# Two edits to a hand-ordered attention-and-MLP kernel: later rounding of raw weights at the seam, and later loads for the last projection block

## The chip, the cores and the metric

The kernel runs on one core of a Trainium2 chip. The metric is the device time of one execution in microseconds (us). Engines are named as in the profile: PE (matmul; PEld its weight loads), DVE (vector), ACT (scalar, activation functions), POOL (GpSimd), SP (which here only issues DMAs). Each engine executes its instructions in the order in which the program emitted them, and waits on semaphores for the others.

## The reference

The input is one sequence of 2048 tokens with 576 features, all in 32-bit floats. Output: a gate between full attention (32 heads of 18) and an MLP.

```
g = sigmoid((x * gate_w).sum(-1))
a = softmax(q @ k.T * 18**-0.5) @ v   per head, then @ wo
b = gelu(layernorm(x) @ w1 + b1) @ w2 + b2      # 576 -> 4608 -> 576
return g * a + (1 - g) * b
```

## The kernel before, in words

Every matrix is used as a rounded high part and the remainder as a low part (the "rounding": an ACT copy to the high part, line 381, then a POOL subtraction for the low part, line 385, booked under the helper's line 176). Products are sums of three matmuls.

**Stages.** Stage A goes over the 4 blocks of 512 input tokens: transposes, q/k projections (groups 0 to 8 of a block, `qk_group`), v projections (groups 9 to 16, `v_group`: even token halves are evicted by ACT, lines 843 and 845, odd ones by DVE, line 847, and stored by SP, line 850), layer-norm outputs y to DRAM. Then comes the main loop: 32 units (16 pairs of heads times 2 halves of the queries) of 16 key chunks each, so 512 steps. A step has score matmuls with exponentials (`s2`, lines 263 and 266), rounds that find row maxima for later units (`s1_round`, lines 223 and 225), and every second step the product with V (`pv`, line 281). Into the gaps between these goes the MLP, a generator whose pieces are pulled one at a time by `fill`; after the MLP the output projection `out_proj` is pulled in the same way. The **seam** is the passage from stage A to the main loop; the **tail** is what follows the last `pv`.

**Slots.** `run_due` counts slots. In stage A it is called by a table: in the last token block once after each of the groups 0 to 8 and twice after each of 9 to 16 (13 slots have passed before that block). In the loop there are 8 slots in two steps, beginning with slot 39. `defer(n, fn)` runs `fn` n slots later. `run_due` also looks through the list `bg` of pieces of background work; one is run when its slot has come and a model of POOL's backlog (sum of modelled operation times minus modelled present) is under its limit: 950 ns for a W1 rounding, 3800 ns for a W2 rounding.

**Raw weights.** In the first token block of the MLP the raw weights are loaded (`load_w1`, line 352, one pair of 128 hidden columns; `load_w2`, line 362, one row chunk), rounded by `split`, used, and stored rounded in DRAM for the other three blocks. One raw buffer R1 serves all W1 pairs, two buffers R2 serve W2 chunks. `LOADED` holds the slot from which a load counts as landed. Only emission order hangs on that slot: the copy itself waits for the transfer, and as ACT runs in order, all that was emitted behind the copy waits too. When a rounding's subtraction is emitted, the load of the next raw piece is deferred by some slots (line 387). The first raw loads are issued within group 2 of the last block; the list is filled at group 9 with W1 0, W2 0 to 3, W1 1 and W1 2. Within group 16 four loads (line 132, `big<-y_scr`) bring the rest of y.

At the seam, PE takes turns between MLP pairs (`h_pair`, matmuls of line 473, two PSUM banks), scores (five banks in rotation) and `pv`. GELU of a pair is a chain of POOL (adds and products), ACT (square, tanh, lines 526 and 524) and POOL steps; its results feed `out_pair` (line 561).

**Tail.** The last unit's `o_store` takes its sums with a copy to DVE's tile `oe`, extracts the denominators (`dn<-oe`, on ACT's queue for the last unit), and 4 slots later `spread` takes the reciprocal (line 305), stores it (line 306) and calls the hook `over`. From then on `ended` is set, outputs leave through ACT's queue, and `load_rest` loads the last rows and denominators of the third and fourth token blocks (lines 1011 and 1016). These two blocks hold the last unit's queries.

`out_proj` works on four blocks of 512 tokens; each has 8 half tiles of 14 matmuls (line 1114, two PSUM banks `ps_w`), evicted by DVE (line 1118) together with gate and MLP result `bt`. Behind each eviction a stage of `normed` for the next block may be emitted, by the table `PLAN`: multiply by the reciprocal denominators (line 1040, DVE), copy (1043, 1046, 1047, ACT), subtract (1050, 1052, DVE). At the start of block b the loads of `bt` for b + 1 are issued, and at the start of block 1 also the attention rows (`load_o(3)`, lines 974 and 977) and denominators (`load_den(3)`, lines 996 and 999) of the fourth block.

Of the kernel before, what the change touches and what calls it, by code (L numbers as in the profile page):

```python
# [23 lines left out]
NB = 4  # L24
# [16 lines left out]
LAND = 8  # L41
# [24 lines left out]
def gated_mix_kernel(ctx: ExitStack, tc: tile.TileContext, x, wqkv, wo, w1, b1, w2, b2, gate_w, out):  # L66
# [68 lines left out]
    slot = [0]  # L135
# [3 lines left out]
    def defer(n, fn):  # L139
        later.append((slot[0] + n, fn))  # L140
# [38 lines left out]
    NU = 2 * NPAIR  # L179
# [108 lines left out]
    def o_store(u, ps):  # L288

        pair, half = unit(u)  # L290
        oe = asm.tile([P, TB], F32, name="oe", bufs=1)
        dn = asm.tile([P, 16], F32, name="dn", bufs=1)
        nc.vector.tensor_copy(oe, ps)
        cols = slice(2 * pair * DH, 2 * (pair + 1) * DH)
        queue = nc.sync if u < NU - 1 else nc.scalar
        queue.dma_start(dn, oe[DH::32, :])
        for h in range(2):
            for qb in range(2):
                c = 32 * (2 * h + qb)
                d = (2 * pair + h) * DH  # L300
                q = half * HALF + qb * TB
                queue.dma_start(ot_scr[0, d:d + DH, q:q + TB], oe[c:c + DH, :])

        def spread():
            nc.vector.reciprocal(dn, dn)
            nc.sync.dma_start(dn_scr[u], dn)
            if u < NU - 1:
                defer(16 if u < NU - 2 else 4, wide)
            else:
                hooks[0]()  # L310

        def wide():
            dst = ot_scr[1, cols, half * HALF:(half + 1) * HALF]
            nc.sync.dma_start(dst.rearrange("(h d) n -> h d n", d=DH), dn_scr[u][:, None, :].to_broadcast([2, DH, HALF]))
            stored.append(u)
        defer(20 if u < NU - 2 else 4, spread)

    rounds = [(u, r) for u in range(NU) for r in range(NR)]
    rounds.reverse()
# [12 lines left out]
    def mlp():  # L332
# [16 lines left out]
        LOADED = {}  # L349
        NQ0 = npair // NB  # L350

        def load_w1(q):

            if (1, q) in LOADED or q >= NQ0:
                return
            LOADED[1, q] = slot[0] + (LAND if looped[0] else LAND - 2)
            fc = chunk(q)[2]
            for h in range(2):
                src = w1[:, (fc + h) * P:(fc + h + 1) * P]
                nc.sync.dma_start(R1[64 * h:64 * h + 64], src.rearrange("(c p) n -> p c n", p=64))  # L360

        def load_w2(c):
            if (2, c) in LOADED or c >= NFC:
                return
            LOADED[2, c] = slot[0] + (LAND if looped[0] else LAND - 2)
            nc.sync.dma_start(R2[c % 2], w2[c * P:(c + 1) * P, :])

        def rounded(dst, src):
# [7 lines left out]
        def split(table, key, pool, shape, raw, src, scr, then):  # L376

            def first():
                LOAD[raw[0]](raw[1])
                t = pool.tile(shape, F32R, name="w" + str(len(shape)))  # L380
                nc.scalar.activation(t[:, 0], src, AF.Copy)  # L381
                bg.insert(0, (any_time, lambda: second(t), queue, 0))

            def second(t):
                pool_op(src.free_size(), nc.gpsimd.tensor_tensor, t[:, 1], src, t[:, 0].bitcast(F32), op=ALU.subtract)
                defer(4 if looped[0] else 26 if raw[0] == 1 else 44, lambda: nc.sync.dma_start(scr, t.bitcast(F32)))
                defer(3 if looped[0] else 2 if raw != (1, 2) else 14, lambda: then(raw[1]))
                table[key] = (t[:, 0], t[:, 1])

            queue = raw[0] ** 2 * SLOT  # L390
            bg.append((lambda: LOADED.get(raw, slot[0] + 1), first, queue, (ROOM if raw[1] > 3 else 0) if raw[0] == 1 else D))
# [552 lines left out]
    def out_proj():  # L944
# [24 lines left out]
        def load_o(b):  # L969

            inflow[0] = slot[0]
            o = x_tile().rearrange("p (c n) -> p c n", c=5)
            cols = slice(b * TB, (b + 1) * TB)
            nc.sync.dma_start(o[:, 0:4, :], ot_scr[0, 0:512, cols].rearrange("(c p) n -> p c n", p=P))
            for h in range(2):
                e = 64 if b < 2 else LAST
                nc.sync.dma_start(o[64 * h:64 * h + e, 4, :], ot_scr[0, 512:512 + e, cols])
            OT[b] = [o]
            done[b] = 0

        def load_den(b):

            while len(stored) < (NU - 2 if b < 2 else NU - 1):
                run_due()
            if b == 0:
                wide = low.bitcast(F32)[:, 0:4, :]
                den = [low.bitcast(F32)[:, c, :] for c in range(5)]
            elif b % 2 == 0:
                wide = KA[0].bitcast(F32).rearrange("p (c n) -> p c n", c=4)
                den = [wide[:, c, :] for c in range(4)] + [QA[2][:, :TB].bitcast(F32)]  # L990
            else:
                tile_ = io.tile([P, 5, TB], F32, name="den", bufs=1)
                wide = tile_[:, 0:4, :]
                den = [tile_[:, c, :] for c in range(5)]
            cols = slice(b * TB, (b + 1) * TB)
            nc.sync.dma_start(wide, ot_scr[1, 0:512, cols].rearrange("(c p) n -> p c n", p=P))
            for h in range(2):
                e = 64 if b < 2 else LAST
                nc.sync.dma_start(den[4][64 * h:64 * h + e], ot_scr[1, 512:512 + e, cols])
            OT[b].append(den)  # L1000
            if ended[0]:
                load_rest(b)
# [3 lines left out]
        def load_rest(b):  # L1006

            o, den = OT[b][:2]
            cols = slice(b * TB, (b + 1) * TB)
            for h in range(2):  # L1010
                nc.sync.dma_start(o[64 * h + LAST:64 * h + 64, 4, :], ot_scr[0, 512 + LAST:576, cols])
            sums = dn_scr[NU - 1][:, (b - 2) * TB:(b - 1) * TB]
            for h in range(2):
                for j in range(2):
                    r = 64 * h + LAST + j * DH
                    nc.sync.dma_start(den[4][r:r + DH], sums[j:j + 1, :].to_broadcast([DH, TB]))
            ready.add(b)

        def load_b(b):
            t0 = len(BT.setdefault(b, []))  # L1020
            bt = io.tile([P, 4 - t0, D], F32, name="bt", bufs=2)
            nc.sync.dma_start(bt, b_scr[b * TB + t0 * P:(b + 1) * TB, :].rearrange("(t p) d -> p t d", p=P))
            BT[b] += [bt[:, t] for t in range(4 - t0)]
# [34 lines left out]
        def over():  # L1058

            ended[0] = True  # L1060
            for b in (2, 3):
                if b in OT and len(OT[b]) > 1:
                    load_rest(b)
        hooks.append(over)
        waiting = []

        def go_on(last):
# [23 lines left out]
        load_b(0)  # L1091
        yield 0
        for b in range(NB):
            if b + 1 < NB:
                load_b(b + 1)
            if b == 1:
                load_o(3)
                load_den(3)
            for t in range(4):
                if b == 0 and t == 1:  # L1100
                    load_o(2)
                    load_den(2)
                tt = 4 * b + t
                tok = slice(t * P, (t + 1) * P)
                res = io.tile([P, D], F32, name="res", bufs=6)
                for n in range(2):
                    cs = slice(n * ND, (n + 1) * ND)
                    ps = psum(ps_w)
                    k = 0
                    for c in range(5):  # L1110
                        while done[b] <= c:
                            run_due()
                        for s_, w_ in ((c, 0), (c, 1), (4 + c, 0)) if c < 4 else ((8, 0), (8, 1)):
                            nc.tensor.matmul(ps[:, :ND], OT[b][2][:, s_, tok], w_part(w_, c)[:, cs], start=(k == 0), stop=(k == 13))  # L1114
                            k += 1
                            if k < 14:
                                yield 122.5
                    nc.vector.scalar_tensor_tensor(res[:, cs], ps[:, :ND], gate[:, tt:tt + 1], BT[b][t][:, cs],
                                                   op0=ALU.mult, op1=ALU.add)
                    if b + 1 < NB:  # L1120
                        waiting.extend((b + 1, stage) for stage in PLAN[b][2 * t + n])
                        go_on(t == 3 and n == 1)
                    yield 122.5
                if ended[0]:
                    nc.scalar.dma_start(out[tt * P:(tt + 1) * P, :], res)
                else:

                    defer(3, lambda res=res, tt=tt: nc.sync.dma_start(out[tt * P:(tt + 1) * P, :], res))
# [100 lines left out]
```

## Time and profile before

| what | us |
|---|---|
| median of 3 runs | 2252.6 (2252.51 to 2253.47) |
| the profiled execution | 2251.12 |
| its span in the profile | 2249.3 |
| granted TensorE clock, mean | 0.997 |
| PE busy | 2223.9 |
| DVE busy | 1648.3 |
| ACT busy | 1425.8 |
| POOL busy | 964.4 |

Rows of a timeline give start, duration, engine, line, operation, output<-inputs, shapes, count of merged instructions, and in brackets the idle time before with what ended it. Rows "A <- B" of the waits give the total, the number and the longest. Rows by stretch give the stretch, then busy time and count of PE, PEld, DVE, ACT and POOL, then the granted TensorE clock, the DMA share and GB/s. DMA rows on SP and ACT's queue show when a transfer was issued, not when it landed.

### The profile page before, as it was taken

The numbers are of one execution on the slowest core, as the hardware profiler recorded it, in microseconds if no ns is written. First come the engines' busy times: TensorE is split into PE (matmuls) and PEld (weight loads), VectorE is DVE, ScalarE is ACT, GpSimd is POOL, SyncE is SP. The second block draws the span as 40 slices with busy tenths as digits, with TensorE's granted clock in tenths as the row PEclk, the third lists the DMA queues.
The fourth block names the chain that finished last, engine by engine and source line by source line (L and its number), as shares of the span: only waits on it lengthen the run. The fifth ranks groups of instructions, "written<-read, shape, count | busy, mean of one in ns | idle before, by whom it ended". The sixth has DMA issues, their size and how long they took to land.

```text
span 2249.3 us, 51651 instructions
## 1 busy us (share of the span) xinstructions
PE 2223.9 (99%) x20585; PEld 1585.0 (70%) x20585; DVE 1648.3 (73%) x2892; ACT 1425.8 (63%) x2650; POOL 964.4 (43%) x970
## 2 busy tenths in 40 slices
PE   9999999999999999999999999999999999999998
PEld 7887666766667677666676666776776767766668
DVE  5677577777778777777777777777776777777734
ACT  4223677777767666666666666666665666666671
POOL 3001666666655444444444444444444444444700
PEclk9999999999999999999999999999999999999999
DMA  8747654445465524333354424232464334232264
GB/s 252 250 171 236 194 173 153 144 157 161 136 204 158 174 83 156 105 131 110 111 156 155 139 78 139 99 122 99 124 171 144 108 120 126 94 134 99 96 201 165
DMA packets 163624, 327.65 MB, mean 146 GB/s; under 512 B 56742, under 2 KB 83978, under 8 KB 152654
## 3 DMA queue, kind: packets, MB, share of 16 engines
q1 hardware_dynamic: 161430, 320.90, 43.7%
q8 instruction: 162, 2.65, 0.5%
q10 hardware_dynamic: 1824, 3.40, 0.4%
q14 instruction: 80, 0.66, 0.1%
q0 software_dynamic: 128, 0.03, 0.0%
HBM read 231.90 MB, written 96.16 MB: 146 GB/s over the span
## 4 chain that ended last, share of the span: by engine, by line
PE 92%; DVE 2%; POOL 2%; DMA 2%; ACT 1%; issue 1%; SPq 1%; POOLq 0%; DVEq 0%; ACTq 0%
PE ps L281 20%; PE ps L473 19%; PE ps L561 19%; PE ps L263 13%; PE ps L223 11%; PE ps L815 4%; PE ps L1114 3%; PE ps L836 2%; DVE m L225 1%; PE ps L742 1%; POOL zz L176 1%; ACT zz L526 0%; DMA low<-ot_scr 0%; PE ps L818 0%; PE ps L817 0%
## 5 line engine op out<-in xcount | busy, mean ns | idle before, releaser
L225 DVE TENSOR_REDUCE m<-ps 128x1 f32<-128x512 f32 x2048 | 1312.4, 684 | 412.2 <-PE ps L223 389.4
L266 ACT ACTIVATE p<-ps 128x512 f32<-128x512 f32 x1368 | 741.2, 596 | 379.6 <-PE ps L263 376.1
L473 PE MATMUL ps<-big,w 64*128 64x512 f32 x3708 | 569.3, 393 | 2.6 <-ACT v L845 1.6
L176 POOL TENSOR_SCALAR zz<-zz 128x512 f32<-128x512 f32 x288 | 178.4, 619 | 751.1 <-ACT zz L526 731.7
L266 ACT ACTIVATE ring<-ps 128x512 f32<-128x512 f32 x680 | 369.0, 596 | 189.1 <-PE ps L263 187.6
L561 PE MATMUL ps<-w,hh 64*128 64x288 f32 x4352 | 483.6, 294 | 2.2 <-DVE x L578 1.3
L263 PE MATMUL ps<-qa,ka 56*128 56x512 f32 x2048 | 459.1, 422 | 5.3 <-ACT p L266 4.8
L561 PEld LDWEIGHTS ps<-w,hh 64*128 64x128 f32 x4352 | 423.8, 186 | 30.4 <-DVE x L578 3.7
L223 PE MATMUL ps<-ka,qa 54*128 54x512 f32 x2048 | 432.6, 398 | 0.7
L473 PEld LDWEIGHTS ps<-big,w 64*128 64x128 f32 x3708 | 367.1, 187 | 71.9 <-ACT v L845 1.9
L176 POOL TENSOR_TENSOR zz<-zz,z 128x512 f32<-128x512 f32 x288 | 371.9, 1291 | 24.0
L263 PEld LDWEIGHTS ps<-qa,ka 56*128 56x128 f32 x2048 | 212.6, 184 | 224.3 <-DVE m L225 180.1
L561 PE MATMUL ps<-w,hl 64*128 64x288 f32 x2176 | 348.1, 292 | 0.8 <-POOL hl L176 0.8
L281 PE MATMUL ps<-p,vt 128*32 128x512 f32 x2560 | 322.8, 598 | 0.0
L223 PEld LDWEIGHTS ps<-ka,qa 54*128 54x128 f32 x2048 | 217.9, 185 | 24.8 <-DVE m L225 3.8
L561 PEld LDWEIGHTS ps<-w,hl 64*128 64x128 f32 x2176 | 231.2, 184 | 1.2 <-POOL hl L176 1.1
L176 POOL TENSOR_TENSOR w<-x,w 128x576 fp32r<-128x576 f32 (+1 forms) x54 | 98.7, 1842 | 299.4 <-ACT w L381 266.7
L176 POOL TENSOR_TENSOR hl<-zz,hh 128x512 fp32r<-128x512 f32 x136 | 176.7, 1299 | 11.4
L281 PE MATMUL ps<-ring,vt 128*32 128x512 f32 x1280 | 168.7, 598 | 0.0
L281 PEld LDWEIGHTS ps<-p,vt 128*32 128x32 f32 x2560 | 67.0, 109 | 142.5 <-issue 136.3
L578 DVE SCALAR_TENSOR_TENSOR x<-ps,x 128x288 f32<-128x288 f32 x256 | 104.1, 448 | 8.6 <-PE ps L561 8.4
L815 PE MATMUL ps<-big,wqk 128*128 128x512 f32 x432 | 109.3, 401 | 0.6 <-DVE wqk L737 0.5
(114 smaller groups left out, 1472.5 us busy)
## 6 DMA issues: line engine op xcount, KB each, us to landing
w<-w_scr SPq DMA_DIRECT2D x54, 1152.0 KB
w<-w_scr SPq DMA_DIRECT2D x108, 576.0 KB
x<-in_B_w_dram SPq DMA_DIRECT2D x72, 288.0 KB
w_scr<-w SPq DMA_DIRECT2D x18, 1152.0 KB
w_scr<-w SPq DMA_DIRECT2D x36, 576.0 KB
qa<-qk_scr SPq DMA_DIRECT2D x192, 72.0 KB
ka<-qk_scr SPq DMA_DIRECT2D x84, 144.0 KB
qk_scr<-hh SPq DMA_DIRECT2D x36, 256.0 KB
```

Of the source, the lines that this page charges most:

```text
L176: fn(*args, **kw)
L223: nc.tensor.matmul(ps, qa[r0:r0 + 54, t * P:(t + 1) * P], ka[r0:r0 + 54, kb * TB:(kb + 1) * TB], start=True, stop=True)
L225: nc.vector.tensor_reduce(M4[u][:, h, t, kb:kb + 1], ps, axis=AX.X, op=ALU.max)
L263: nc.tensor.matmul(ps[h], ka[r0:r0 + 56, kc * P:(kc + 1) * P], qa[r0:r0 + 56, qb * TB:(qb + 1) * TB], start=True, stop=True)
L266: nc.scalar.activation(RING[n % 3][:, qb, h], ps[h], AF.Exp, scale=SCALE)
L281: nc.tensor.matmul(OB[u][r:r + 32, :], v[:, k, 19 * h:19 * h + 32], RING[c % 3][:, qb, h, :], start=(k == 0), stop=(k == NT - 1))
L473: nc.tensor.matmul(ps[h], wt[w_][r, c, :], y[r, c, :], start=(k == 0), stop=(k == 26))
L561: mm = nc.tensor.matmul(ps[nn][:, :ND], h_[r, tok], w_[p_][r, cs[nn]], start=(k == 0), stop=(k == 6 * G - 1))
L578: nc.vector.scalar_tensor_tensor(dst, ps[nn][:, :ND], 0.5, b2b[:, cs[nn]] if g == 0 else dst, op0=ALU.mult, op1=ALU.add)
L815: nc.tensor.matmul(ps, w_[:, c, ms], big[:, s_, :], start=(k == 0), stop=False)
L836: nc.tensor.matmul(ps[:, :ND], big[:, s_, tok], w_[:, c, cs], start=(k == 0), stop=False)
L1114: nc.tensor.matmul(ps[:, :ND], OT[b][2][:, s_, tok], w_part(w_, c)[:, cs], start=(k == 0), stop=(k == 13))
```

## The change

At the seam, two things: a load issued before the main loop counts as landed after 8 slots (`LAND`) instead of 6, and the next load is deferred by 3 slots behind a rounding instead of 2 (the case of 14 for W1 2 stays). In the loop both numbers were 8 and 3 already.

In the tail, two things: the last unit's `spread` is deferred by 2 slots instead of 4, and the loads of `bt` for the third block and of the attention rows and denominators for the fourth are no longer issued at the start of block 1, but held and issued at the end of the hook `over`, that is behind the store of the last denominators and behind `load_rest(2)`; `load_rest(3)` follows within `load_den(3)`. If the hook has already run when block 1 starts, they are issued there as before.

```
-        defer(20 if u < NU - 2 else 4, spread)
+        defer(20 if u < NU - 2 else 4 if u < NU - 1 else 2, spread)
...
-            LOADED[1, q] = slot[0] + (LAND if looped[0] else LAND - 2)
+            LOADED[1, q] = slot[0] + LAND
...
-            LOADED[2, c] = slot[0] + (LAND if looped[0] else LAND - 2)
+            LOADED[2, c] = slot[0] + LAND
...
-                defer(3 if looped[0] else 2 if raw != (1, 2) else 14, lambda: then(raw[1]))
+                defer(3 if looped[0] else 3 if raw != (1, 2) else 14, lambda: then(raw[1]))
...
                     load_rest(b)
+            while held:
+                held.pop()()
         hooks.append(over)
+        held = []
+
+        def last_loads():
+            load_b(2)
+            load_o(3)
+            load_den(3)
...
         for b in range(NB):
-            if b + 1 < NB:
+            if b == 1 and not ended[0]:
+                held.append(last_loads)
+            elif b == 1:
+                last_loads()
+            elif b + 1 < NB:
                 load_b(b + 1)
-            if b == 1:
-                load_o(3)
-                load_den(3)
```

## The prediction

> **What bounds the kernel now.** The busy line of the page comes first, then PE's own waits, longest first.
>
> ```profile
> PE 2223.9 (99%) x20585; PEld 1585.0 (70%) x20585; DVE 1648.3 (73%) x2892; ACT 1425.8 (63%) x2650; POOL 964.4 (43%) x970
> PE ps L263 <- ACT p L266: 4.8, 9, 3.0
> PE ps L1114 <- DVE big L1050: 3.8, 1, 3.8
> PE ps L473 <- ACT v L845: 1.6, 1, 1.6
> ```
>
> PE is busy all through, so only PE's idle time and PE's slow time can be won. Two of these waits stand at the seam (L473, and the 3.0 of L263), one in the tail (L1114), and each long one has a sequel, which the busy times by stretch show in the clock column.
>
> ```profile
> 230.00:235.00 5.00, 2.01 (x11) 1.01 (x8) 1.07 (x2) 3.03 (x5) 1.79 (x1) 0.83 1.09 235
> 235.00:240.00 5.00, 4.77 (x19) 1.71 (x22) 1.95 (x3) 1.93 (x4) 1.61 (x3) 0.50 0.80 204
> 2210.00:2215.00 5.00, 1.63 (x4) 1.03 (x4) 3.01 (x5) 1.15 (x2) 0.00 (x0) 0.80 0.49 149
> 2215.00:2220.00 5.00, 4.90 (x21) 4.93 (x22) 1.80 (x4) 0.63 (x1) 0.00 (x0) 0.52 0.84 295
> ```
>
> After 2.99 us idle at the seam and 3.81 in the tail the granted clock falls to half: 0.17 x 5 + 0.50 x 5 = 3.4 us lost at each place, beside the idle time.
>
> **The seam: who is late.** Rows of the timeline on ACT, SP, POOL and PE.
>
> ```profile
> 220.27 2.46 ACT L381 ACTIVATE w<-x 128x576 fp32r<-128x576 f32 x3 [4.94 <-DMA x<-in_B_w_dram]
> 223.01 1.08 ACT L266 ACTIVATE p<-ps 128x512 f32<-128x512 f32 x2
> 231.97 1.16 ACT L381 ACTIVATE w<-x 128x1152 fp32r<-128x1152 f32 x1 [4.08 <-DMA x<-in_B_w_dram]
> ...
> 222.47 1.70 SPq L366 DMA_DIRECT2D x<-in_B_w_dram  x2
> 226.47 1.46 SPq L360 DMA_DIRECT2D x<-in_B_w_dram  x2
> 227.98 2.59 SPq L132 DMA_DIRECT2D big<-y_scr  x4
> ...
> 221.04 5.41 POOL L176 TENSOR_TENSOR w<-x,w 128x576 fp32r<-128x576 f32 x3 [6.70 <-DMA x<-in_B_w_dram]
> ...
> 223.17 0.96 PE L473 MATMUL ps<-big,w 64*128 64x512 f32 x6 [1.59 <-ACT v L845]
> 224.20 0.40 PE L263 MATMUL ps<-qa,ka 56*128 56x512 f32 x2
> 230.28 0.40 PE L263 MATMUL ps<-qa,ka 56*128 56x512 f32 x1
> 233.67 0.79 PE L263 MATMUL ps<-qa,ka 56*128 56x512 f32 x1 [2.99 <-ACT p L266]
> 240.82 0.50 PE L263 MATMUL ps<-qa,ka 56*128 56x512 f32 x2
> ```
>
> ACT runs in order. A rounding copy (L381) that comes up before its raw weights have landed holds everything behind it: 4.94 us before the three copies at 220.27, so that the V copies of group 15 are late and PE idles 1.59; then 4.08 us before the copy at 231.97 (the third pair, W1 2), behind which the exponentials stand, so that PE finds no free score bank for 2.99.
>
> **The seam: what the edit moves.** I count slots by the rules in the code: one slot after groups 0 to 8 of the last input block, two after 9 to 16. The first raw loads go out at slot 15, the rounding list is made at slot 22. With 8 slots instead of 6, W1 0 and W2 0 become due at 23, and the list is first looked at in slot 23: no change, nor for W2 1 in slot 24. The next loads move from slots 25 and 26 to 26 and 27, past no other transfer of SP, so they start when they do now. Their roundings move from 31, 32 and 34 to 34 (W2 2), 35 (W2 3) and 37 (W1 1): POOL's modelled backlog then lets them through one by one. So group 15's V copies stand behind one copy instead of three. Loads of W2 4 and W2 5 go from slots 33, 34 to 37, 38, and W1 2's load from 36 to 40: all three pass behind the four loads of y (L132), which are issued inside group 16. W1 2 is due at 48 instead of 42; in 48 to 50 POOL's modelled backlog is over the 950 ns allowed (2.1 to 2.5 us), in 51 it is 0.2, so it is rounded in slot 51, behind the first GELU steps of the first pair.
>
> The costs. The same three copies and the V copies still run on ACT ahead of the first exponential, from the same landing, so that one stays at 223.01 and frees its bank at about 223.6; PE's second score pair (224.20 now, its second matmul 0.12 later) cannot end sooner. Hence the 1.59 shrinks by only 0.7. From there ACT has nothing to wait for. Now the y loads, and PE's pieces at full clock, from the chain of waits:
>
> ```profile
> 229.97 6.31 DMA big<-y_scr
> 242.26 0.93 PE ps L473 x8
> 243.19 0.24 PE ps L263 x2
> 249.01 1.85 PE ps L281 x16
> ```
>
> The y loads need only PE's end of group 16, 221.6 at the latest (223.17 - 1.59), not 227.98. Issued in 2.59, the last of them starts its way at about 223.5 and lands within 6.31, by 229.9; PE wants the first at about 229.8. PE then needs 7.11 (223.17 to 230.28) plus 0.24 + 0.93 + 0.24 + 1.85 = 3.26 to the score pair after the first P.V, 10.37 in all; now it takes 240.82 - 223.17 = 17.65. Gain 7.28 + 0.7 = **8.0 us**.
>
> Against it stands W1 2 at its new place.
>
> ```profile
> 233.21 2.63 POOL L176 TENSOR_TENSOR w<-x,w 128x1152 fp32r<-128x1152 f32 x1 [6.76 <-ACT w L381]
> 253.60 0.62 POOL L176 TENSOR_SCALAR zz<-zz 128x512 f32<-128x512 f32 x1 [0.36 <-DVE m L225]
> 257.62 0.63 ACT L524 ACTIVATE zz<-zz 128x512 f32<-128x512 f32 x1
> 267.07 0.43 PE L561 MATMUL ps<-w,hh 64*128 64x288 f32 x4
> ```
>
> Its copy (1.16) and subtraction (2.63) now delay POOL's GELU chain by up to 3.8. The first output matmul (267.07) is far enough, but the second pair's first step (253.60) slips to about 257.0, and the tanh behind it (257.62) then holds ACT's exponentials for some 1.4. Bounds: 0, and 2.63 + 3.4 = 6.1 if the third pair's matmuls must wait for the subtraction and the clock falls. The five score banks take part of the 1.4, so I take 1.0. Net **-7.0 us**.
>
> **The tail.** Rows on DVE, on SP, ACT's issue, one of SP's waits, and a stretch in which the queue was full.
>
> ```profile
> 2200.18 0.24 DVE L305 RECIPROCAL dn<-dn 128x16 f32<-128x16 f32 x1
> ...
> 2206.58 0.52 DVE L1118 SCALAR_TENSOR_TENSOR res<-ps,gate,bt 128x288 f32<-128x288 f32 x1
> 2211.91 0.69 DVE L1040 TENSOR_TENSOR x<-x,qa 128x512 f32<-128x512 f32 x1 [4.81 <-DMA qa<-dn_scr]
> ...
> 2243.78 0.52 DVE L1118 SCALAR_TENSOR_TENSOR res<-ps,gate,bt 128x288 f32<-128x288 f32 x1 [1.34 <-PE ps L1114]
> 2245.64 0.52 DVE L1118 SCALAR_TENSOR_TENSOR res<-ps,gate,bt 128x288 f32<-128x288 f32 x1 [1.34 <-PE ps L1114]
> 2191.26 0.38 SPq L1022 DMA_DIRECT2D bt<-b_scr  x1
> ...
> 2200.84 0.38 SPq L996 DMA_DIRECT2D den<-ot_scr  x1
> ...
> 2202.86 0.79 SPq L306 DMA_DIRECT2D dn_scr<-dn  x1
> ...
> 2209.01 1.34 SPq L1016 DMA_DIRECT2D qa<-dn_scr  x4
> 2195.29 1.12 ACTq L296 DMA_DIRECT2D dn<-oe  x1
> SPq L996 <- DMA x<-ot_scr: 3.9, 1, 3.9
> 2160.00:2180.00 20.00, 20.00 (x144) 12.52 (x143) 6.20 (x11) 14.27 (x28) 0.00 (x0) 1.00 1.02 347
> ```
>
> A half tile takes 1.86 (the last two L1118). From 2206.58 there are 17 more: they could end at 2206.58 + 31.62 = 2238.20 and end at 2245.64: **7.44 us** lost, which is the 3.81, two crumbs and the slow clock. The last denominators are late: dn_scr<-dn leaves at 2202.86 behind the fourth block's den loads, takes 6.15 us behind them (to 2209.01), and DVE stands at 2211.91.
>
> Now the spread is two slots (18 matmuls) after the last P.V, so the reciprocal stands just ahead of the second L1118 of block 1 on DVE and waits for dn<-oe. With the queue empty that needs about the 1.6 of a small transfer (four qa loads: 2.9 from first issue to use, 1.34 of it issuing): reciprocal at 2197.4, dn_scr at 2197.6, landed by 2200.0 if it takes 2.4; even with 6.15 the sums would be usable at 2206.7, and they are wanted at 2207.0. The wait falls; 0.3 us may stay for the last rows' conversion.
>
> What is late next: bt, o and den of the fourth block are queued on SP behind the qa loads, which wait for dn_scr. They start at 2201.35. Three loads of 1152 + 1024 + 1024 KB and four of 56 KB are 3.51 MB: at the full queue's 347 GB/s 10.1 us, landing 2211.5. From above: bt and o took from 2191.26 to 2200.84, when den's issue had waited 3.9 for o's landing; with 8.2 more for den (2200.84 to 2209.01 bounds it) that is 17.8, landing 2219.1. Three output stores of 0.29 MB share the queue (2.5 us), giving 2214.0; the middle of the ends is 2215.3. I take 2215. DVE wants den for the fourth block behind the first L1118 of the third block (2210.30 + 0.44); stuck there, it evicts the second half tile at 2215.6 to 2216.1, and PE, which has two banks, stands from 2213.9 to 2216.15: 2.25. That lies between 1.59 (full clock after it) and 2.99 (half clock), nearer the first: no slow clock. Tail: 7.44 - 0.3 - 2.25 = **-4.9 us**.
>
> The Trainium skill, "DMA: Bandwidth & Descriptors", section "Anatomy of one DMA — SWDGE (gpsimd) path", gives a transfer 2.0 us plus its bytes at 436 GB/s; an estimate by it has den landed at 2211.4 and the sum 2.25 lower, while bt and o here took 9.6 us for what it prices at 7.1.
>
> **Sum.** The profiled execution took 2251.12 (span 2249.3): 2251.1 - 7.0 - 4.9 = 2239.2. The median of the runs is 1.5 higher: **2240.7**.
>
> **Rivals.** (a) den is in time: landing 2211.5, DVE waits 0.7, PE not; 2238.5. For it: 347 GB/s was held for 20 us with these same tensors. (The Trainium skill's figure from "DMA: Bandwidth & Descriptors" gives this case.) (b) The tail gains nothing: the loads are issued one upon another's landing as the row with 3.9 shows, den at 2219.1, PE idle 6.3 plus 3.4 plus 0.3 against 7.44, 2.6 worse: 2248.2. Against it: small transfers now stand ahead of den, long landed. (c) The seam's wait only moves: W1 2's subtraction is late for the third pair, 8.0 - 6.1 = 1.9 gained: 2245.8. Against it: in slot 51 it stands eight POOL operations (the first pair's closing GELU steps) ahead of the second pair's first step, about when PE begins the third pair. (b) and (c) together: 2253.3. (d) Slower: each W1 load of the first token block leaves three slots after the rounding before it, so the whole chain runs late and all 15 later pairs wait. If each exposes its ACT copy of 1.16, 17.4 are lost: 2258.1; it decides from 11.9 / 15 = 0.8 us a pair. Against it: W1 3 isn't wanted until after the first group's outputs.
>
> **Chances.** Forecast 0.42, (a) 0.20, (b) 0.15, (c) 0.13, both 0.05, (d) 0.05. Within 0.2% (4.5 us, about what a measurement can tell) lie half of (b), a little of (c) and the pair: 0.13. Slower 0.06, faster 0.81. The likeliest case alone spans 2238.5 to 2244 (the tail stall with a slow clock); the range down to (a) with no cost at the seam and up past (b): 2237 to 2249.
>
> **What would show it.** At the seam: ACT's copy of W1 2 starts without idle time before it, y loads on SP near 221, granted clock 1.00 from 225 to 240, PE's L263 wait of 2.99 gone and about 0.9 left ahead of an early L263. In the tail: dn_scr near 2198 (less the seam's gain), no wait of L1114 for L1050, DVE waiting at L1040 for den, and a PE wait for L1118's bank of about 2. I am wrong if PE waits at the third pair, if the half clock returns, or if PE's idle time between 300 and 2150 grows.

## The result, and the profile after

The changed kernel takes 2245.55 us, the median of 9 runs (2243.22 to 2248.87), against 2252.51 (2251.82 to 2253.87) for the kernel before on the same chip: 7.0 us less, a ratio of 0.997 with a 95% interval of 0.9959 to 0.998. Forecast were 2240.7 and a gain of 11.8. The sign is right and the time lies in the range; the likeliest case was 4.9 us too good. The runs of the new kernel also lie further apart: 5.7 us, where the kernel before has 2.1. They order by the mean granted TensorE clock: 1.000 in the fastest run, 0.999 in the next four, 0.998 in the four slowest (0.002 of 2245 us is 4.5 us).

The profiled execution took 2244.72, its span 2242.9 (2249.3 before). First the busy line of its page, then PE's waits from the view that groups them (in total, times, longest).

```profile
PE 2220.6 (99%) x20585; PEld 1588.3 (71%) x20585; DVE 1648.7 (74%) x2892; ACT 1425.8 (64%) x2650; POOL 964.2 (43%) x970
...
PE ps L263 <- ACT p L266: 2.4, 9, 0.7
PE ps L561 <- DVE x L578: 2.4, 4, 1.4
PE ps L1123 <- DVE res L1127: 2.1, 1, 2.1
PE ps L561 <- POOL hh L176: 1.6, 2, 0.8
PE ps L473 <- ACT v L845: 1.0, 1, 1.0
```

(The projection's matmul and eviction are L1123 and L1127 now; they were L1114 and L1118.) The two long waits, 3.0 for p and 3.8 for big, are gone. In their place stand 2.1 for a bank in the tail, which was forecast, and two that were not: 1.4 for DVE's L578, and a second 0.8 for POOL's hh (the kernel before has one, and none over 0.4 for L578). The same kernel by stretches; the third number from the right is the granted clock.

```profile
230.00:235.00 5.00, 5.00 (x43) 2.83 (x43) 3.23 (x5) 3.20 (x6) 1.23 (x2) 1.00 1.14 306
235.00:240.00 5.00, 5.00 (x46) 4.05 (x44) 2.58 (x4) 3.99 (x8) 3.14 (x4) 1.00 0.06 26
...
2140.00:2145.00 5.00, 3.87 (x33) 3.69 (x35) 4.98 (x10) 2.52 (x5) 0.76 (x1) 0.75 0.16 37
2145.00:2150.00 5.00, 5.00 (x55) 3.36 (x53) 3.85 (x7) 5.00 (x11) 1.12 (x1) 0.91 0.57 179
2210.00:2215.00 5.00, 2.94 (x22) 2.70 (x21) 1.40 (x3) 0.23 (x1) 0.00 (x0) 1.00 0.69 258
2215.00:2220.00 5.00, 5.00 (x39) 5.00 (x39) 4.87 (x10) 2.31 (x5) 0.00 (x0) 1.00 0.80 256
```

The seam (230 to 240) and the tail (2210 to 2220) run at full clock in this execution. A slow stretch stands at a new place, 2140 to 2150: 0.25 x 5 + 0.09 x 5 = 1.7 us lost.

Where the 6.4 us of span come from is read off the starts of the P.V matmuls (L281) in both traces, counted in sets of 16 (two key chunks):

| set of P.V matmuls | before | after | difference |
|---|---|---|---|
| 0 (seam) | 237.89 | 232.23 | -5.66 |
| 2 | 257.44 | 250.69 | -6.75 |
| 8 | 306.19 | 301.20 | -4.99 |
| 200 | 1784.53 | 1779.70 | -4.83 |
| 246 | 2135.52 | 2131.14 | -4.38 |
| 248 | 2148.86 | 2147.10 | -1.76 |
| end of the span | 2249.3 | 2242.9 | -6.4 |

So the seam gave 6.7 (at set 0 the kernel before still had slow clock ahead of it), of which 1.8 was lost again by set 8 and 0.6 over the long middle; 2.6 went within two sets near 2140, and the tail gave 4.6.

**The seam, row by row** (timeline of the changed kernel: ACT, PE, SP):

```profile
220.01 0.69 ACT L381 ACTIVATE w<-x 128x576 fp32r<-128x576 f32 x1 [4.76 <-DMA x<-in_B_w_dram]
221.93 0.42 ACT L843 ACTIVATE vt<-ps 128x288 f32<-128x288 f32 x1 [1.24 <-DMA v_scr<-vt]
...
222.32 1.74 ACT L381 ACTIVATE w<-x 128x576 fp32r<-128x576 f32 x2
223.94 2.06 ACT L266 ACTIVATE p<-ps 128x512 f32<-128x512 f32 x4
238.20 1.17 ACT L381 ACTIVATE w<-x 128x1152 fp32r<-128x1152 f32 x1
...
222.49 0.97 PE L473 MATMUL ps<-big,w 64*128 64x512 f32 x6 [0.99 <-ACT v L845]
224.59 0.49 PE L263 MATMUL ps<-qa,ka 56*128 56x512 f32 x1 [0.68 <-ACT p L266]
234.08 0.50 PE L263 MATMUL ps<-qa,ka 56*128 56x512 f32 x2
...
221.09 2.54 SPq L132 DMA_DIRECT2D big<-y_scr  x4
```

One copy, not three, stands ahead of group 15's V copies, the y loads are issued at 221.09, and the copy of W1 2 at 238.20 waits for nothing, all as forecast. But the V copy at 221.93 now waits 1.24 for something that was not in the forecast: its buffer vt is free only when the store of it has landed. The first exponential starts at 223.94, not 223.01, and PE pays 0.68 for it. Behind W1 2's subtraction GpSimd is late at the first output matmuls (POOL and PE):

```profile
239.45 2.68 POOL L176 TENSOR_TENSOR w<-x,w 128x1152 fp32r<-128x1152 f32 x1 [1.69 <-ACT w L381]
261.54 1.03 PE L561 MATMUL ps<-w,hh 64*128 64x288 f32 x4 [0.84 <-POOL hh L176]
```

**The start of the projection** (DVE and PE). The normalization of the first block is queued on DVE ahead of its denominators' landing; DVE stands at it for 7.95 us, and the evictions L578 behind it come so late that PE, out of banks, idles 1.45. The first two rows are the kernel before at the same place, the others the changed kernel.

```profile
2143.28 0.69 DVE L1040 TENSOR_TENSOR x<-x,low 128x512 f32<-128x512 f32 x1 [6.83 <-DMA low<-ot_scr]
2144.40 0.89 PE L561 MATMUL ps<-w,hh 64*128 64x288 f32 x4 [0.35 <-DVE x L578]
...
2140.02 0.69 DVE L1040 TENSOR_TENSOR x<-x,low 128x512 f32<-128x512 f32 x1 [7.95 <-DMA low<-ot_scr]
2140.62 0.82 DVE L578 SCALAR_TENSOR_TENSOR x<-ps,x 128x288 f32<-128x288 f32 x2
2141.13 0.89 PE L561 MATMUL ps<-w,hh 64*128 64x288 f32 x4 [1.45 <-DVE x L578]
```

**The tail** (DVE, SP, PE):

```profile
2195.31 0.25 DVE L305 RECIPROCAL dn<-dn 128x16 f32<-128x16 f32 x1 [1.28 <-DMA dn<-oe]
2204.66 0.52 DVE L1127 SCALAR_TENSOR_TENSOR res<-ps,gate,bt 128x288 f32<-128x288 f32 x1
2213.60 0.69 DVE L1040 TENSOR_TENSOR x<-x,den 128x512 f32<-128x512 f32 x1 [4.04 <-DMA x<-ot_scr]
2239.25 0.52 DVE L1127 SCALAR_TENSOR_TENSOR res<-ps,gate,bt 128x288 f32<-128x288 f32 x1 [1.34 <-PE ps L1123]
...
2195.59 0.33 SPq L306 DMA_DIRECT2D dn_scr<-dn  x1
...
2208.49 0.37 PE L1123 MATMUL ps<-big 128*128 128x288 f32 x1 [0.41 <-DVE big L1052]
2214.77 1.60 PE L1123 MATMUL ps<-big 128*128 128x288 f32 x10 [2.06 <-DVE res L1127]
```

The denominators leave as soon as the reciprocal is done; 0.41 remains at the third block, and the fourth block's loads are late in their turn: DVE stands 4.04 at L1040, PE 2.06. (The row at 2213.60 names `x<-ot_scr`, but the trace has the last landing of den at 2213.50, just ahead of it; with the loads in the same order the rows of the kernels with the fourth normalization later and with the spread at 4 slots name den.) From the eviction at 2204.66 to the last one 34.59 us pass, where the kernel before took 2245.64 - 2206.58 = 39.06 for the same seventeen half tiles: 4.5 won.

### The profile page after: what moved, and what is told of

Same layout as the page of the kernel before. It is cut to its first block, busy times and chain, and to the rows that moved or that the text cites. A ratio compares the mean times of both kernels' runs of the same rounds, so it can differ in the third digit from the quotient of the medians.

```text
span 2242.9 us, 51659 instructions
## 1 busy us (share of the span) xinstructions
PE 2220.6 (99%) x20585; PEld 1588.3 (71%) x20585; DVE 1648.7 (74%) x2892; ACT 1425.8 (64%) x2650; POOL 964.2 (43%) x970
## 4 chain that ended last, share of the span: by engine, by line
PE 92%; DVE 2%; DMA 2%; POOL 1%; ACT 1%; SPq 0%; issue 0%; ACTq 0%; DVEq 0%; POOLq 0%
PE ps L281 20%; PE ps L473 20%; PE ps L561 19%; PE ps L263 13%; PE ps L223 11%; PE ps L815 4%; PE ps L836 2%; PE ps L1123 2%; DVE m L225 1%; DMA x<-ot_scr 1%; PE ps L742 1%; DMA low<-ot_scr 0%; POOL zz L176 0%; ACT zz L526 0%; PE ps L818 0%
## 5 line engine op out<-in xcount | busy, mean ns | idle before, releaser
L473 PE MATMUL ps<-big,w 64*128 64x512 f32 x3708 | 570.0, 393 | 1.8 <-ACT v L845 1.0
L473 PEld LDWEIGHTS ps<-big,w 64*128 64x128 f32 x3708 | 370.9, 187 | 66.7 <-ACT v L845 1.3
L281 PE MATMUL ps<-p,vt 128*32 128x512 f32 x2560 | 322.8, 598 | 0.0
L281 PE MATMUL ps<-ring,vt 128*32 128x512 f32 x1280 | 168.5, 598 | 0.0
L281 PEld LDWEIGHTS ps<-p,vt 128*32 128x32 f32 x2560 | 67.0, 109 | 142.6 <-issue 136.4
L578 DVE SCALAR_TENSOR_TENSOR x<-ps,x 128x288 f32<-128x288 f32 x256 | 104.1, 448 | 9.6 <-PE ps L561 9.6
```

Source lines behind the costliest of these rows:

```text
L281: nc.tensor.matmul(OB[u][r:r + 32, :], v[:, k, 19 * h:19 * h + 32], RING[c % 3][:, qb, h, :], start=(k == 0), stop=(k == NT - 1))
L473: nc.tensor.matmul(ps[h], wt[w_][r, c, :], y[r, c, :], start=(k == 0), stop=(k == 26))
L578: nc.vector.scalar_tensor_tensor(dst, ps[nn][:, :ND], 0.5, b2b[:, cs[nn]] if g == 0 else dst, op0=ALU.mult, op1=ALU.add)
```

## The experiments

Theory: seam and tail give their gains independently; what is missing was given back at three places, by the store of vt and GpSimd's chain at the seam, by DVE at the projection's start, and by chance halvings of the clock behind each short idle time. Main rivals: that the later W1 chain costs in the middle, and that only one half of each edit does the work. Each ratio is against the kernel before, run beside it on the same chip. Where two kernels ran on different chips, the column "less than before" compares them better than the medians do.

| kernel | median, us | less than before | ratio, 95% interval |
|---|---|---|---|
| the changed kernel | 2245.55 | 7.0 | 0.9970 (0.9959 to 0.9980) |
| seam alone | 2247.99 | 4.8 | 0.9977 (0.9968 to 0.9987) |
| tail alone | 2250.00 | 2.8 | 0.9989 (0.9981 to 0.9998) |
| first block's normalization later | 2243.56 | 9.2 | 0.9962 (0.9948 to 0.9975) |
| fourth block's normalization later | 2241.54 | 11.2 | 0.9953 (0.9940 to 0.9965) |
| both normalizations later | 2240.92 | 11.6 | 0.9950 (0.9937 to 0.9962) |
| and W1 2 subtracted on VectorE | 2239.45 | 13.1 | 0.9943 (0.9930 to 0.9955) |
| and 9 slots before the loop | 2238.56 | 14.9 | 0.9934 (0.9922 to 0.9947) |
| or W2's loads 8 slots behind | 2241.74 | 11.8 | 0.9948 (0.9934 to 0.9962) |
| changed, spread at 4 slots | 2248.31 | 4.3 | 0.9981 (0.9972 to 0.9990) |
| changed, loads not held | 2249.88 | 2.7 | 0.9987 (0.9978 to 0.9996) |
| changed, 2 slots behind a rounding | 2243.96 | 9.5 | 0.9959 (0.9947 to 0.9972) |
| changed, 6 slots before the loop | 2247.63 | 5.9 | 0.9972 (0.9962 to 0.9982) |

**Seam alone.** The kernel before with the three edited lines of the seam.

> The kernel before with the seam's part of the change alone: 8 slots for all loads, 3 slots behind a rounding, the tail as it was. Theory (the two parts add, and what is given back comes after the seam): 5.7 us are won up to the first P.V, 0.7 given back at the first output matmuls, another 0.6 in the last 400 us, and the start of the output projection may or may not cost its 1.45 idle and 1.7 of slow clock; the tail loses its 7.4 as before. 2252.5 - 4.4 = 2248.1, up to 2250.8 with that stall. Rival (the later W1 chain costs in the middle): the offset to the kernel before shrinks steadily from 300 us on. Rival (the changed seam is what makes the projection's start stall): that stall is in this profile, and not in that of the tail's part alone.

2247.99, as the theory said. Its P.V matmuls come 5.4 us early at set 0, 4.8 at sets 16 and 32, 5.1 at 128, 4.4 at 240: no steady shrinking, so the later W1 chain costs nothing in the long middle. About 0.4 goes between sets 192 and 208. It goes there in the profiles with both of the seam's edits as they stand, and not with the tail's alone or with one of the two. PE's idle time between these sets is 0.5 in the changed kernel and in the one before, so the loss lies in the length of its rows; why stays open. At the projection's start PE waits 1.1 for L578 here and 0.8 with the tail's edit alone, each without a slow clock, so these two runs do not settle which edit lengthens that wait.

**Tail alone.** The changed kernel with the seam's lines put back.

> The changed kernel with the seam's part undone: 6 slots for loads of before the loop, 2 slots behind a rounding; held loads and the spread two slots behind the last P.V stay. Theory: every P.V at the time of the kernel before, seam and projection's start as before (2.99 us wait and slow clock at the seam; DVE held by the first block's denominators for about 7 us, PE idle under 0.5), the tail 4.5 us shorter: 2248.0. Rival (the tail's gain needs the earlier arrival of the loop): under 3 us won.

2.8 won, not 4.5. The seam waits as before, and in the tail the wait is longer than in the first profile (PE's waits):

```profile
PE ps L263 <- ACT p L266: 5.1, 9, 3.3
...
PE ps L1123 <- DVE res L1127: 2.9, 1, 2.9
```

The two parts add: 4.8 + 2.8 = 7.6 beside 7.0 for both. The rival's number, under 3 us, came, but its reason is not borne out: where the loop does arrive earlier, the tail's edit wins no more (from 4.8 to 7.0). Each alone falls short of its forecast of 7.0 and 4.9.

**First block's normalization four slots later.**

```
-            defer(4 + 2 * c, lambda c=c: normed(0, c))
+            defer(8 + 2 * c, lambda c=c: normed(0, c))
```

> The changed kernel with the first block's normalization put four slots later (8 + 2c in place of 4 + 2c), so that on VectorE its first product stands behind two more evictions of L578 and behind the copy of oe. Theory (VectorE, held by the first block's denominators, is what idles PE 1.45 us near 2141, and with it what halves the clock for 3.4 us): DVE's wait at L1040 falls from 7.95 to about 1, PE's wait for L578 goes, the clock stays 1.00 to 2200: 2245.5 - 2.7 = 2242.8, and the runs lie closer together. Rival (the clock falls there for another reason): the half clock stays, under 1 us won. Rival (the wait only moves): PE waits for big at the first projection matmuls, about 2155, for 2 us or more.

On DVE two evictions and the copy of oe now stand ahead of the first L1040, which no longer waits:

```profile
2139.30 0.69 DVE L293 COPY oe<-ps 128x512 f32<-128x512 f32 x1 [1.14 <-PE ps L281]
2139.90 0.68 DVE L1040 TENSOR_TENSOR x<-x,low 128x512 f32<-128x512 f32 x1
```

PE's longest wait for L578 is 0.3, the clock is 1.00 from 2135 to 2160, and no wait came up at the projection's first matmuls. That much is shown. The time, 2.0 less than the changed kernel's median, is not apart from it by the intervals, and the runs lie as far apart as before (2241.56 to 2246.28): the spread has other sources as well.

**Fourth block's normalization one half tile later.**

```
-        [(0,), (1,), (2,), (3,), (4,), (5,), (6,), ()]]
+        [(), (0,), (1,), (2,), (3,), (4,), (5,), (6,)]]
```

> The changed kernel with the fourth block's normalization begun one half tile later in the third block's plan. Theory (PE's 2.06 us wait in the tail is DVE held at L1040 until den of the fourth block lands at about 2213.5): L1040 now stands behind one more eviction and waits about 1.6 instead of 4.04, PE's wait of 2.06 goes, and at the fourth block's first half tile up to 0.4 comes back, because its last product is one half tile nearer: 2245.5 - 1.7 = 2243.8. Rival (the normalization is too late there): PE waits for big of the fourth block for 1 us or more, nothing won.

L1040 waits 2.42, now behind one more eviction, and PE 0.5 in place of 2.06 and more. Against the changed kernel the median is 4.0 less, over twice the 1.7 that was expected (the intervals just overlap). The likely reason is that in other executions the wait had cost slow clock too, which the profile of the estimate did not show; the five profiles compared below bear this out.

**Both.**

> Both edits on the changed kernel: the first block's normalization four slots later, the fourth block's one half tile later. Theory (two places, each with its own idle time and its own chance of a slow clock): the gains add, 2245.5 - 4.0 - 2.0 = 2239.5, PE's waits for L578 near 2141 and for L1127 near 2214 both under 0.7, the clock at 1.00 at both; what lottery remains is the seam's (PE idle 1.2 to 1.7 near 222, a slow clock of 3.4 us behind it in some runs). Rival (they share one cause): 2241.5, no better than the second alone.

2240.92: at both places PE waits 0.6 or less and the clock is full. Over the fourth block's edit alone it is 0.6 better, inside the scatter; whether the two gains add, the times do not tell.

**W1 2 subtracted on VectorE**, on top of both.

```
-                pool_op(src.free_size(), nc.gpsimd.tensor_tensor, t[:, 1], src, t[:, 0].bitcast(F32), op=ALU.subtract)
+                if raw == (1, 2):
+                    nc.vector.tensor_tensor(t[:, 1], src, t[:, 0].bitcast(F32), op=ALU.subtract)
+                else:
+                    pool_op(src.free_size(), nc.gpsimd.tensor_tensor, t[:, 1], src, t[:, 0].bitcast(F32), op=ALU.subtract)
```

> The former, with the subtraction of W1 2 alone on VectorE in place of GpSimd. Theory (W1 2's subtraction, 2.7 us on GpSimd in the middle of the first pair's GELU steps, is what makes PE wait 0.84 for hh at the first output matmuls): that wait goes, the offset to the kernel before stays at -6.7 up to the hundredth step instead of falling to -5.0, 1.0 to 1.7 us won: 2238.2. Rival (hh is late for other reasons, as the first exponentials are): nothing won. Rival (DVE is short there): PE's wait for DVE z grows by about the 1.3 that the subtraction takes.

PE's waits for hh fall from two (1.6 in all) to one, the one that the kernel before has too (its lines stand three later):

```profile
PE ps L564 <- POOL hh L176: 0.8, 1, 0.8
```

From set 0 to set 100 it needs 776.39 us where the former needs 777.56: 1.2 won, and DVE, where the subtraction takes 2.21, keeps nobody waiting longer. The median is 1.5 lower; the intervals overlap.

**Which half of the tail's edit.** The spread back at four slots, or the loads not held:

```
-        defer(20 if u < NU - 2 else 4 if u < NU - 1 else 2, spread)
+        defer(20 if u < NU - 2 else 4, spread)
```

> The changed kernel with the spread of the last unit back at four slots; the fourth block's loads stay behind its denominators. Theory (both halves of the tail's edit are needed): the reciprocal comes 3 us later, and with it all loads behind it, den of the fourth block lands at about 2216.5 instead of 2213.5, PE stands about 5 us for it and gets the slow clock: 2245.5 + 3 + 3.4 = 2251.9. Rival (putting the loads behind is all that counts): 2245.5 to 2246.5.

```
-            if b == 1 and not ended[0]:
-                held.append(last_loads)
-            elif b == 1:
-                last_loads()
-            elif b + 1 < NB:
+            if b + 1 < NB:
                 load_b(b + 1)
+            if b == 1:
+                load_o(3)
+                load_den(3)
```

> The changed kernel with the fourth block's loads issued where the kernel before has them, and the spread at two slots. Theory (the denominators are late because they stand behind those loads): dn<-oe lands in 4 to 5 us instead of 1.9, DVE is held at the reciprocal for it, dn_scr takes about 6 us in the full queue, PE still waits 2 to 4 us for the third block's big and may lose clock, den of the fourth block is in time: 2248.5, between the two kernels' tails. Rival (the earlier spread alone is the gain): 2245.5 or less, because the fourth block's wait is gone as well.

Neither half alone wins anything over the seam alone: 4.3 and 2.7 less than the kernel before, where the seam alone has 4.8. With the spread late, the fourth block's denominators are late too, and DVE waits 7.31 for them in place of 4.04 (DVE, PE):

```profile
2213.90 0.69 DVE L1040 TENSOR_TENSOR x<-x,den 128x512 f32<-128x512 f32 x1 [7.31 <-DMA den<-ot_scr]
2215.08 2.77 PE L1123 MATMUL ps<-big 128*128 128x288 f32 x10 [5.32 <-DVE res L1127]
```

The wait of 5 us and the slow clock behind it are as expected; 2251.9 was too high, in part probably because it was counted from a median that already holds some slow clock. With the loads ahead, the early reciprocal itself waits for dn in the full queue and holds DVE, and the third block's big is late as before:

```profile
2197.91 0.25 DVE L305 RECIPROCAL dn<-dn 128x16 f32<-128x16 f32 x1 [3.69 <-DMA dn<-oe]
2198.56 1.59 PE L1122 MATMUL ps<-big 128*128 128x288 f32 x10 [1.17 <-DVE res L1126]
2212.34 0.53 PE L1122 MATMUL ps<-big 128*128 128x288 f32 x2 [3.16 <-DVE big L1050]
```

**Which half of the seam's edit.** 2 slots in place of 3 behind a rounding:

```
-                defer(3 if looped[0] else 3 if raw != (1, 2) else 14, lambda: then(raw[1]))
+                defer(3 if looped[0] else 2 if raw != (1, 2) else 14, lambda: then(raw[1]))
```

> The changed kernel with 2 slots in place of 3 behind a rounding, so the 8 slots alone of the seam's edit. The loads of W2 4 and W2 5 then stand ahead of the loads of y on SP and hold them until GpSimd has subtracted W2 2 and W2 3; the copies of W2 2 and W2 3 both stand ahead of group 15's V copies. Theory (the 8 slots win the seam, because they alone take W1 2's copy out of the exponentials' way; V is held by the store of vt anyway): PE's long wait for p stays away, y comes 0 to 1.5 us late at about 230, W1 2 one slot earlier relieves the first outputs a little: 2246, 2245 to 2248. Rival (the third slot is what wins): the wait of 3 us for p, or one as long for y, and the slow clock are back, 2250 or more.

6 slots in place of 8 (for `load_w1` and `load_w2`):

```
-            LOADED[2, c] = slot[0] + LAND
+            LOADED[2, c] = slot[0] + (LAND if looped[0] else LAND - 2)
```

> The changed kernel with 6 slots for loads of before the loop, so the third slot alone of the seam's edit. W2 2, W2 3 stand ahead of group 15's V copies, W1 2's copy stands behind the first eight exponentials with its load issued about as late as in the changed kernel. Theory (a copy that comes up before its landing holds the exponentials): ACT waits 2 to 4 us at W1 2's copy, PE 1 to 3 us for p, with a slow clock in some runs: 2248, 2246.5 to 2251. Rival (the third slot wins the seam): no such wait, 2245.5.

With 8 slots alone all of the gain is there (2243.96, below the 2245 to 2248 expected; the interval overlaps with the changed kernel's). With the third slot alone ACT is held by the raw W1 2 again, for 6.26 where the kernel before has 4.08, and PE behind it for 2.16 (first ACT, then PE):

```profile
235.46 1.16 ACT L381 ACTIVATE w<-x 128x1152 fp32r<-128x1152 f32 x1 [6.26 <-DMA x<-in_B_w_dram]
...
237.16 0.50 PE L263 MATMUL ps<-qa,ka 56*128 56x512 f32 x1 [2.16 <-ACT ring L266]
```

So the 8 slots are enough for the seam's gain. The third slot alone is not worth nothing: with it the gain is 5.9, with neither, in the tail alone, 2.8, and the two intervals only just touch. Added to the 8 slots it wins nothing that these runs can tell.

**What holds group 15's V copies.** On the kernel with W1 2 on VectorE, 9 slots before the loop (for both loads):

```
-            LOADED[2, c] = slot[0] + LAND
+            LOADED[2, c] = slot[0] + (LAND if looped[0] else LAND + 1)
```

> The kernel with both normalizations later and W1 2's subtraction on VectorE, with 9 slots before the loop: group 15's V copies now stand ahead of the copy of W2 2 and of its wait for the raw weights. Theory (V is late for the store of vt, which lands at about 221.8 behind the four raw loads, and not for the copy ahead of it): L381's 4.8 us wait moves behind the V copies or goes, V copies still start at about 221.9, PE's waits of 0.7 to 1.4 for v and 0.7 for p stay: 2239.5, within 0.5. Rival (the copy of W2 2 holds V): V copies at 219.5, both waits gone, 2237.8.

With no copy ahead of it the V copy still starts when the store has landed:

```profile
221.28 0.42 ACT L846 ACTIVATE vt<-ps 128x288 f32<-128x288 f32 x1 [6.15 <-DMA v_scr<-vt]
...
221.67 1.26 ACT L381 ACTIVATE w<-x 128x576 fp32r<-128x576 f32 x2
222.81 1.09 ACT L266 ACTIVATE p<-ps 128x512 f32<-128x512 f32 x2
```

The store, then, not the copy of W2 2; the rival's 219.5 did not come. The median is 0.9 lower (1.8 when each is set against the kernel before beside it), inside the scatter. But the store landed a little earlier and two copies, not three, stand ahead of the first exponential (222.81): PE's wait for v fell to 0.5 and the 0.7 for p went, which the theory had denied. By its median this is the fastest kernel of the study.

**W2's loads behind the store.** Again on the kernel with W1 2 on VectorE:

```
-                defer(3 if looped[0] else 3 if raw != (1, 2) else 14, lambda: then(raw[1]))
+                defer(3 if looped[0] else 8 if raw[0] == 2 else 3 if raw[1] < 2 else 14, lambda: then(raw[1]))
```

> The same kernel with 8 slots, and before the loop W2's loads 8 slots behind the rounding before them in place of 3, W1's still 3: on SP the loads of W2 2 and W2 3 now stand behind the store of group 13's vt, and their roundings come up among the first exponentials; W1 1's copy comes ahead of group 15's V copies, W1 2's some slots earlier. Theory (the store of vt behind the raw loads is what makes V and the first exponentials late): the store lands by about 219.5, V copies by about 220.2, the first exponentials at about 221.5, PE's waits for v (0.7 to 1.4) and for p (0.7) go, and with them the chance of a slow clock at the seam: 2239.4 - 1.8 = 2237.6. Rival (the roundings moved among the exponentials hold them in turn): PE waits for p 1 us or more between 223 and 232, nothing won or 1 to 3 us lost.

```profile
219.70 0.40 ACT L846 ACTIVATE vt<-ps 128x288 f32<-128x288 f32 x1
...
221.47 1.09 ACT L266 ACTIVATE p<-ps 128x512 f32<-128x512 f32 x2 [1.28 <-PE ps L263]
...
233.05 1.16 ACT L381 ACTIVATE w<-x 128x1152 fp32r<-128x1152 f32 x1 [5.00 <-DMA x<-in_B_w_dram]
...
234.75 0.50 PE L263 MATMUL ps<-qa,ka 56*128 56x512 f32 x1 [2.12 <-ACT ring L266]
```

V at 219.70 and the exponentials at 221.47 are what the theory gave, and both waits are gone. The loss is the rival's, a little later than it said: W1 2's copy now comes up 5 us ahead of its landing, PE idles 2.12, and the clock halves behind it. The median is 2.3 us worse than that of the kernel that it started from, 1.3 when each is set against the kernel before beside it; the intervals overlap, so the loss is read from the trace and not from the times.

## Why the prediction was right, and where it was not

**The direction and the mechanisms hold.** ACT's copies came up before their raw weights; given more slots, the 2.99 and its slow clock are gone. The last denominators stood behind the fourth block's loads; put ahead, the 3.81 is gone. Rival (d), a loss over the later pairs, fell with the flat offset of the seam's kernel; rival (a) with L1040's wait of 4.04; rival (c) with the 238.20 copy, which nothing waits for at the third pair. Two rivals' times are nearer to the measured one than the forecast is, by luck and not by their mechanism: 2245.8 of (c) (its bound, 2.63 + 3.4, is 6.0 and not 6.1), whose wait is not there, and 2248.2 of (b), though the tail did gain and den landed where the forecast had it (2213.50, with the 1.8 us by which this tail begins earlier 2215.3). The time also lies outside the 2238.5 to 2244 given for the likeliest case alone. And two of the prediction's own signs of being wrong came, both near 2141: the half clock returned for 3.41 us, and PE's idle time between 300 and 2150, the gaps between its rows, grew from 5.8 to 6.8 us (up to 2100 it is the same, 5.4).

**The seam's 8.0 was mis-sized: 6.7.** The step that failed is "that one stays at 223.01": the first exponential came at 223.94. The V copies were costed as held by the rounding copies alone; they also wait for the store of vt, queued behind four raw loads. The 0.7 won at L473 is given back as 0.68 at the second score pair, and some 0.5 more lies in PE's own pieces, which took a little longer than the chain's rows.

**W1 2's place was taken at 1.0 and cost 1.8.** The delay of GpSimd's chain by its 2.68 was seen, but put on ACT's exponentials, with the sentence that "the first output matmul (267.07) is far enough". It is not, once all before it has moved up by 6.7 and GpSimd's chain has not: it comes at 261.54 and waits 0.84; another 0.7 of the 1.8 lies in longer rows of PE. In the kernel with this subtraction on VectorE the offset stays at 5.1 from set 2 to set 8, so the whole 1.8 hangs on the subtraction's place; up to set 2 that kernel gains 0.5 less than the one with both normalizations later, hence 1.2 by set 100.

**The tail's 4.9 was mis-sized: 2.8.** The landing and the wait are right: den lands within 0.3 of the 2215 forecast, and PE waits 2.06 (2.25 forecast); the 2.4 taken for dn_scr's way, for which no row was given, was 1.8. The estimate of 2211.4 that the prediction worked out from the Trainium skill, "DMA: Bandwidth & Descriptors", was 4 us early; the section that it cites is on DMAs that GpSimd issues, and these loads are issued by SP. "No slow clock" is not right. Five profiles hold the same tail code. Beside the row of the changed kernel above (1.60 for ten matmuls behind a wait of 2.06) stand those of the tail alone, of the first normalization later, of 2 slots behind a rounding, and of 6 slots before the loop:

```profile
2220.64 1.60 PE L1123 MATMUL ps<-big 128*128 128x288 f32 x10 [2.87 <-DVE res L1127]
```
```profile
2211.89 2.74 PE L1123 MATMUL ps<-big 128*128 128x288 f32 x10 [2.17 <-DVE res L1127]
```
```profile
2214.21 2.77 PE L1123 MATMUL ps<-big 128*128 128x288 f32 x10 [3.04 <-DVE res L1127]
```
```profile
2217.67 2.57 PE L1123 MATMUL ps<-big 128*128 128x288 f32 x10 [2.89 <-DVE res L1127]
```

Ten matmuls take 1.60 at full clock and about 2.7 with the clock halved. Three of five were slowed: the granted clock from 2200 to 2225 is 0.93, 0.86 and 0.93 in the last three, so some 1.7, 3.4 and 1.7 us are lost. The mean over the five is 2.6 of wait and 1.4 of clock; with the 0.4 at L1052 that makes 7.44 - 4.4 = 3.0 won, as the tail alone shows (2.8). The wait should have had a price for the clock by chance, not a yes or no by its length.

**The middle was costed at nothing.** DVE's wait for the first block's denominators stood in the trace of before too (6.83 us, PE 0.35) and was not priced as something that the shift could lengthen. In the profile shown it took 2.6 with its slow clock; in the other profiles with this normalization PE's wait there was 0.4 to 1.2, with no slow clock. The 2.6 of the table is one execution, not the price.

Added up: 1.3 at the seam, 0.8 for W1 2, 0.6 over the long middle (its cause is open) and 2.1 in the tail are the 4.8 between forecast and median; what the projection's start costs on average lies inside the scatter. That the sum closes is partly luck: its seam comes from one profile and its tail from a median, and the slow clock at the seam, 3.4 and 1.7 us in two of the seven profiles with this seam (0.7 on the mean), is in none of its terms.

## What to carry to other kernels

An engine that runs in order is late with everything behind an instruction whose data has not landed; giving that instruction more slots helps only as far as the next thing it meets, here a buffer's store, another engine's chain, or the next load of the same chain that moves with it. When a stretch is won, list what does not move up with it: those are the next waits. And price an idle time of 1.5 to 3 us on TensorE with a chance of a halved clock behind it; a wait that costs no clock in the one profile at hand can cost some in the median.

## What the runs showed of the hardware

Whether the slow clock follows a short wait differs from execution to execution. The same code with the same wait was followed by it in some executions and not in others, at three places: in the tail after 2.17, 2.89 and 3.04 but not after 2.06 and 2.87; at the seam after 1.3 + 0.7 of waits in the kernel with the fourth normalization later (granted clock 0.86 from 220 to 245) and after 0.9 + 0.7 in the one with the loads not held (0.93), but not in five others with the same code there; near 2141 once, after 1.45. By the clock records of the traces, slow stretches in the middle of a run last 3.41 or 6.83 us, and where a trace has two, they start a whole number of steps of 3.413 us apart (233.28 and 2213.01 in the kernel before: 580 steps).

Cut into these steps, from 205 us to shortly before the end, the fourteen traces show what decides. Of the steps at full clock, all ten in which PE's rows fill 41% or less are followed by a slow step, four of the twenty-two between 52 and 70%, and none of those above. So the tail's 2.17 was followed by a slow clock because it lies in one step (36% busy), and the 2.87 was not because it is cut into two (56 and 60%). What sorts the cases between 52 and 70% stays open. The Trainium skill, "TensorE: Matmul & The Clock Gate", section "What's actually happening", describes a window of 3413 ns that runs freely and is not aligned with the program. The stretches' lengths and spacing agree with it. Its section "HAM oscillation — how this bites in real kernels" warns of gaps over about 3.4 us; here 2.17 sufficed, and once 1.45.

A small store behind large loads is priced by the loads: the store of vt (0.4 MB) landed 2.3 us after its issue where only two other small stores were ahead of it, and 6.0 behind the four raw loads in the changed kernel (1.2 MB); with only two of them ahead, in the last experiment, 4.8. The Trainium skill, "DMA: Bandwidth & Descriptors", section "Queues, rings and completion order", has descriptors consumed in the order of the ring, which agrees.
